# Gate row load moved, one weight block loaded in two pieces, ten weight blocks in one transfer: three edits to the loads of a fused mixing kernel

## The chip, the cores and the metric

The kernel runs on one core of one Trainium2 chip. Time is the device time of one execution in microseconds (us), as the median of several executions. Profiles are of one further execution each. A core has TensorE (matmuls, reading weights and data from the on-chip memory and adding up in eight banks of its own memory), VectorE, ScalarE and GpSimd, and SyncE, whose queue issues most loads. Sixteen DMA engines move the data.

## The reference, cut to what matters

```python
x = A_x                                          # 1 x 2048 x 512, bf16
g = sigmoid((x * gate_w).sum(-1, keepdims=True))
q, k, v = split_heads(x @ wqkv)                  # 32 heads of 16
phi = lambda t: concat(softmax(t @ w_phi), softmax(-(t @ w_phi)))
kv = einsum("bhsf,bhsd->bhfd", phi(k), v); z = phi(k).sum(s)
a = (phi(q) @ kv / (phi(q) @ z + 1e-6)) @ wo
b = relu(x @ w1) @ w2                            # w1 512 x 1376, w2 1376 x 512
return g * a + (1 - g) * b
```

## The kernel before

x is needed with its 512 columns on the partitions, in four chunks of 512 rows. Of chunk 0, TensorE transposes the first 256 columns itself and a transposing load brings the rest; chunks 1 to 3 come by transposing loads. The loads are issued in this order; `p.early` only moves the first ones ahead of the start's barrier.

```python
loadx0("sp", "x00", slice(0, 2), 0)
loadx0("act", "x01", slice(2, 4), 0)
p.dma("act", lambda e: e.dma_start(out=GR[0:NDT, :], in_=gate_w.rearrange("(j p) -> j p", p=P)),
      "gr", after=["grz"], ev="gr")               # the gate row, 1 KB
loadw1(0, 0, 4 * P, "a")                          # W1 block 0, columns 0..511
loadx0("sp", "x02", slice(0, 4), P)
loadw1(0, 4 * P, 8 * P)
for t in (1, 2):
    loadw1(t, 0, 8 * P)                           # W1 blocks 1 and 2, 256 KB each
p.dma("sp", ... e.dma_start_transpose(XT[:, 2:4, 0:512], ...), "x0t")     # chunk 0, columns 256..511
loadw1(3, 0, 8 * P)
p.dma("sp", ... W1[:, :, 8 * P:DFF] ..., "w1r")
p.dma("sp", ... WPS ... A_w_phi ..., "wps")       # w_phi, 16 KB
p.dma("sp", ... WV ..., "wv")                     # value weights, 512 KB
for i in range(2): p.dma("sp", ... e.dma_start_transpose(WQKT[...], ...), f"wqk{i}")  # query, key weights
for c in range(1, NCH): p.dma("sp", ... e.dma_start_transpose(XT[:, :, c * 512:...], ...), f"x{c}")
```

TensorE begins with the first MLP product of chunk 0 in four slabs. A slab takes one block of 128 columns of x and adds to all eight banks:

```python
XV = (("xva", "xvb"), ("xvc", "xvd"), ("x0t",), ("x0t",))
def slab(t, us=range(8)):
    for u in us:
        p.op("pe", lambda e, u=u: e.matmul(PS[:, UB[u], :], W1[:, t, u * P:(u + 1) * P], XT[:, t, 0:512], ...),
             after=["w10a" if t == 0 and u < 4 else f"w1{t}", *XV[t]] + ...)
```

Then it goes on in a fixed order, in which `hunit(1, 0)` is the first work on chunk 1. Everything ahead of it works on chunk 0 or on weights:

```python
hunit(0, 8); hunit(0, 9, "dve"); gatecol(0)
vtile(0, "dve"); vtile(1, "act", nextbank()); vtile(2, "dve")
for i in range(4): pre(i)              # folds w_phi into the query weights
vtile(3, "act", 5); rest(0); atile(0, 0)
for i in range(4, 8): pre(i)           # the same for the key weights
...
hunit(1, 0, "dve")                     # waits for "x1", rows 512..1023 of x
for m in range(NT): atile(m, None if m else 1); ...
    if m == 3:
        for a, b in ((0, 5), (5, KU)): # W2's whole blocks, 640 KB each
            p.dma("sp", ...)
```

The softmax here doesn't subtract the row's maximum and nothing guards it: scores larger than these inputs give would overflow.

## Time and profile before

| | before |
|---|---|
| median, three first runs | 146.74 us (146.73 to 147.30) |
| six runs beside the change | 146.78 us (146.67 to 147.30) |
| span of the profile | 145.3 us |
| TensorE busy | 98% |
| first W1 matmul / last matmul's weight load | 3.45 / 143.03 us |

SyncE's queue in order of time: start, length, queue and line, kind, tile, count.

```profile
3.10 1.34 SPq L176 DMA_TRANSPOSE XT<-in_A_x_dram  x1
...
5.57 0.51 SPq L181 DMA_DIRECT2D WPS<-in_A_w_phi_dram  x1
6.12 0.51 SPq L183 DMA_DIRECT2D WV<-in_A_wqkv_dram  x1
6.67 6.68 SPq L186 DMA_TRANSPOSE PHQ<-in_A_wqkv_dram  x2
13.39 7.58 SPq L189 DMA_TRANSPOSE XT<-in_A_x_dram  x3
```

Each line begins where the one above ends, give or take 0.05 us. These lengths are those of the issue; the data lands later.

### The profile page before, as it was taken

What the parts mean: (1) busy time and instruction counts of PE and PEld (TensorE: products, weight loads), DVE (VectorE), ACT (ScalarE), POOL (GpSimd) and SP (SyncE); (2) the same over time, 40 slices, a digit from 0 to 9 for tenths busy, and PEclk for the clock granted to TensorE, in tenths of its full rate; (3) what the DMA queues carried; (4) which work ended last, traced back from release to release, by engine and by line L of the source; (5) the groups of instructions that cost most, each with busy time, mean ns of one, the idle gap of its engine ahead of it and who ended that gap; (6) DMA issues with size and microseconds to landing.
All of it is one profiled execution on the core that took longest, in us unless ns stands there. A gap on an engine that the chain in (4) does not pass through costs nothing.

```text
span 145.3 us, 2523 instructions
## 1 busy us (share of the span) xinstructions
PE 142.3 (98%) x970; PEld 71.9 (50%) x970; DVE 92.5 (64%) x157; ACT 72.0 (50%) x125; POOL 52.1 (36%) x62
## 2 busy tenths in 40 slices
PE   8999999999999999999999999999999999999994
PEld 3444654454446445645555545554544444444443
DVE  3348557977686888678698968664455555555342
ACT  4124677778878778797878861122111111111150
POOL 2013002977878678678879801200000000000000
PEclk9999999999999999999999999999999999999999
DMA  6999994042359985315334332355142223222213
GB/s 153 250 299 201 251 202 89 0 94 55 72 119 355 154 167 109 70 36 111 77 72 103 78 72 40 80 104 134 49 108 72 72 72 77 72 72 74 72 45 106
DMA packets 47045, 16.12 MB, mean 111 GB/s; under 512 B 41432, under 2 KB 46648, under 8 KB 47032
## 3 DMA queue, kind: packets, MB, share of 16 engines
q1 hardware_dynamic: 46608, 15.85, 48.5%
q8 instruction: 8, 0.13, 0.4%
q10 hardware_dynamic: 424, 0.10, 0.3%
q14 instruction: 5, 0.04, 0.1%
HBM read 4.15 MB, written 2.10 MB: 43 GB/s over the span
## 4 chain that ended last, share of the span: by engine, by line
PE 94%; DMA 3%; DVE 1%; SPq 1%; issue 0%
PE PS L496 26%; PE PS L273 19%; PE PS L352 18%; PE PS L417 10%; PE PS L505 10%; PE PS L533 4%; PE PS L471 3%; PE PS L439 3%; DMA W<-in_B_w_dram 3%; PE PS L285 2%; PE PS L307 1%; DVE WQK L519 1%; SPq L162 0%; SPq L158 0%; PE PS L225 0%
## 5 line engine op out<-in xcount | busy, mean ns | idle before, releaser
L496 PE MATMUL PS<-W,HT 128*128 128x512 bf16 (+4 forms) x187 | 40.6, 366 | 0.0
L385 POOL TENSOR_TENSOR EB<-EB,SC 128x1024 bf16<-128x1024 bf16 x15 | 28.9, 1928 | 22.7 <-DVE SC L383 22.7
L336 ACT ACTIVATE EB<-PS 128x480 bf16<-128x480 f32 (+1 forms) x46 | 30.3, 732 | 13.4 <-PE PS L352 13.4
L510 ACT ACTIVATE TFA<-PS,GT 128x512 bf16<-128x512 f32 x16 | 11.0, 687 | 42.7 <-PE PS L505 36.6
L273 PE MATMUL PS<-XT,W 128*128 128x512 bf16 x128 | 30.9, 379 | 0.0
L352 PE MATMUL PS<-WQK,XT 128*128 128x480 bf16 x128 | 28.7, 366 | 0.0
L519 DVE SCALAR_TENSOR_TENSOR WQK<-PS,OMG,TFA 128x512 bf16<-128x512 f32 (+2 forms) x17 | 12.2, 719 | 23.6 <-ACT TFA L510 22.4
L496 PEld LDWEIGHTS PS<-W,HT 128*128 128x128 bf16 (+1 forms) x187 | 17.1, 98 | 17.4
L381 DVE TENSOR_REDUCE ZB<-EB 128x64 f32<-128x1024 bf16 x15 | 18.3, 1220 | 11.4 <-ACT EB L336 11.4
L259 ACT ACTIVATE HT<-PS 128x512 bf16<-128x512 f32 x34 | 19.8, 615 | 6.9 <-PE PS L533 5.1
L352 PEld LDWEIGHTS PS<-WQK,XT 128*128 128x128 bf16 x128 | 12.4, 98 | 13.8 <-DVE WQK L312 0.4
L396 DVE TENSOR_REDUCE ZB<-EB 128x64 f32<-128x1024 bf16 x16 | 18.6, 1164 | 0.0
L273 PEld LDWEIGHTS PS<-XT,W 128*128 128x128 bf16 x128 | 12.0, 98 | 13.0
L405 POOL TENSOR_TENSOR EB<-EB,SC 128x512 bf16<-128x512 bf16 x16 | 16.9, 1056 | 1.3
L417 PE MATMUL PS<-WV,XT 128*128 128x512 bf16 x64 | 16.2, 378 | 0.0
L505 PE MATMUL PS<-WO,OT 128*128 128x512 bf16 x64 | 16.1, 378 | 0.0
L481 DVE TENSOR_TENSOR WQK<-PS,RDEN 128x512 bf16<-128x512 f32 x16 | 11.1, 692 | 0.6
L427 ACT ACTIVATE VS<-PS 128x512 bf16<-128x512 f32 x14 | 8.5, 610 | 2.3 <-PE PS L417 2.3
L505 PEld LDWEIGHTS PS<-WO,OT 128*128 128x128 bf16 x64 | 6.1, 97 | 7.2
L383 DVE RECIPROCAL SC<-ZB 128x64 f32<-128x64 f32 x16 | 8.8, 553 | 0.5
L533 PE MATMUL PS<-XT,W 128*128 128x512 bf16 x32 | 7.5, 379 | 0.6 <-DMA W<-in_B_w_dram 0.3
L417 PEld LDWEIGHTS PS<-WV,XT 128*128 128x128 bf16 x64 | 5.4, 97 | 5.0 <-DVE VS L425 0.4
(57 smaller groups left out, 84.5 us busy)
## 6 DMA issues: line engine op xcount, KB each, us to landing
out_dram<-WQK SPq DMA_DIRECT2D x15, 128.0 KB, 1.8
W<-in_B_w_dram SPq DMA_DIRECT2D x2, 640.0 KB, 5.4
W<-in_B_w_dram SPq DMA_DIRECT2D x3, 256.0 KB, 3.8
WV<-in_A_wqkv_dram SPq DMA_DIRECT2D x1, 512.0 KB, 5.4
WO<-in_A_wo_dram SPq DMA_DIRECT2D x2, 256.0 KB, 3.4
W<-in_B_w_dram SPq DMA_DIRECT2D x1, 352.0 KB, 4.8
W<-in_B_w_dram SPq DMA_DIRECT2D x2, 128.0 KB, 2.5
PHQ<-EB SPq DMA_TRANSPOSE x16, 2.7
```

Source lines behind the costliest of these rows:

```text
L259: p.op("act", lambda e: e.activation(dst, src, ACT.Relu), after=[f"h{c}_{kt}"], ev=ev)
L273: p.op("pe", lambda e, t=t: e.matmul(PS[:, bank, :], W1[:, t, kt * P:(kt + 1) * P], XT[:, t, c * 512:(c + 1) * 512], start=(t == 0), stop= ...
L336: p.op("act", lambda e: e.activation(dst, s_, ACT.Exp, scale=scale), after=[qk] + busy, ev=ev)
L352: p.op("pe", lambda e, dt=dt, which=which: e.matmul(PS[:, which, 0:DE], XT[:, dt, m * P:(m + 1) * P], WQK[:, which, dt * DE:(dt + 1) * DE] ...
L381: p.op("dve", lambda e: e.tensor_reduce(zk, ek, AX.X, ALU.add), after=[emk, f"cst{b}"], ev=f"zk{m}")
L385: p.op("pool" if m < NT - 1 else "dve", lambda e: e.tensor_tensor(EB[:, b, 3, :].rearrange("p (g f) -> p g f", f=DH), EB[:, b, 2, :].rearr ...
L396: p.op("dve", lambda e: e.tensor_reduce(ZB[:, b, 0:64].rearrange("p (h s) -> p h s", s=2), bass.AP(tensor=EB, offset=base, ap=[[EBS, P], [ ...
L405: p.op("pool", lambda e: e.tensor_tensor(EB[:, b, 0, :].rearrange("p (h s f) -> p h s f", h=H, s=2)[:, :, 1, :], EB[:, b, 1, :].rearrange( ...
L417: p.op("pe", lambda e, dt=dt: e.matmul(PS[:, bank, :], XT[:, dt, m * P:(m + 1) * P], WV[:, dt, :], start=(dt == 0), stop=(dt == NDT - 1)), ...
L496: p.op("pe", lambda e, kt=kt, M=M: e.matmul(PS[:, bank, 0:n], HT[0:M, kt, m * P:(m + 1) * P], W2[0:M, kt, cs], start=(kt == 0), stop=(kt = ...
L505: p.op("pe", lambda e, t=t: e.matmul(PS[:, bank, :], OT[:, t, m * P:(m + 1) * P], WO[:, t, :], start=(t == 0), stop=(t == NDT - 1)), after ...
L519: p.op("dve", lambda e: e.scalar_tensor_tensor(out=OSB[:, ob, cs], in0=PS[:, bank, 0:n], scalar=OMG[:, m:m + 1], in1=TFA[:, m % 2, cs], op ...
```

## The change

The intent: the tiny gate row out of the way of the first loads; the first half of W1's second block early enough that slab 1 needn't wait; one issue less for W2.

```diff
-        p.dma("act", ... GR[0:NDT, :] ... gate_w ..., "gr", after=["grz"], ev="gr")     # at the start
...
-        for t in (1, 2):
-            loadw1(t, 0, 8 * P)
+        loadw1(1, 0, 4 * P, "a")
+        loadw1(1, 4 * P, 8 * P)
+        loadw1(2, 0, 8 * P)
...
-                    after=["w10a" if t == 0 and u < 4 else f"w1{t}", *XV[t]] + ...
+                    after=[f"w1{t}a" if t < 2 and u < 4 else f"w1{t}", *XV[t]] + ...
...
         xev("act", "b", (2, 3), (0,), 7)
+        p.dma("act", ... GR[0:NDT, :] ... gate_w ..., "gr", after=["grz"], ev="gr")
...
-                for a, b in ((0, 5), (5, KU)):
+                for a, b in ((0, KU),):
```

More of the change, by code (lines that the diff above doesn't have):

```diff
@@ L166, in bass_gated_mix__linear_kernel_hedgehog__dense_activation_relu__prompt_kernel @@
         loadx0("act", "x01", slice(2, 4), 0)
-        p.dma("act", lambda e: e.dma_start(out=GR[0:NDT, :], in_=gate_w.rearrange("(j p) -> j p", p=P)),
-              "gr", after=["grz"], ev="gr")
         p.early("act")
@@ L251, in xev @@
             free[bank] = [f"xv{nm}"]
-        w1all = ["w10a", "w1r"] + [f"w1{t}" for t in range(NDT)]
+        w1all = ["w10a", "w11a", "w1r"] + [f"w1{t}" for t in range(NDT)]
         def relu(c, kt, bank, eng):
@@ L535, in slab @@
                     start=(t == 0), stop=(t == NDT - 1)),
-                    after=["w10a" if t == 0 and u < 4 else f"w1{t}", *XV[t]] + (free[UB[u]] if t == 0 else []),
+                    after=[f"w1{t}a" if t < 2 and u < 4 else f"w1{t}", *XV[t]] + (free[UB[u]] if t == 0 else []),
                     ev=(f"h0_{u}" if t == NDT - 1 else None))
@@ L545, in bass_gated_mix__linear_kernel_hedgehog__dense_activation_relu__prompt_kernel @@
         xev("act", "b", (2, 3), (0,), 7)
+        p.dma("act", lambda e: e.dma_start(out=GR[0:NDT, :], in_=gate_w.rearrange("(j p) -> j p", p=P)),
+              "gr", after=["grz"], ev="gr")
         warm(1, 384)
```

## The prediction

> **What bounds the kernel now.** I read the page's shares and chain first, to see which engine sets the end; then the chain in order of time, to see what comes ahead of that engine's stream; then the timeline of the first 23 us; then the DMA issues of short windows, because all three parts of the change are loads.
>
> ```profile
> PE 142.3 (98%) x970; PEld 71.9 (50%) x970; DVE 92.5 (64%) x157; ACT 72.0 (50%) x125; POOL 52.1 (36%) x62
> ...
> PE 94%; DMA 3%; DVE 1%; SPq 1%; issue 0%
> ```
>
> TensorE is busy for 98% of the span and is 94% of the chain that ended last; only 3% of the chain is a DMA. So a load can pay only where TensorE really stands still, and this is at the start. The chain in order of time, from the beginning, shows the one load on it:
>
> ```profile
> 1.60 0.51 SPq L162
> 2.11 0.04 issue
> 2.15 3.71 DMA W<-in_B_w_dram
> 5.86 0.05 issue
> 5.90 5.45 PE PS L533 x24
> ```
>
> The 2.15 us issue is the second block of W1 (rows 128 to 255, columns 0 to 1023, 256 KB), which slab 1 waits for. It landed 3.71 us later, at 5.86. The timeline gives the size of the hole:
>
> ```profile
> 2.92 0.38 ACT L250 ACTIVATE XT<-PS 128x256 bf16<-128x256 f32 x1 [0.22 <-PE PS L238]
> 3.45 0.81 PE L533 MATMUL PS<-XT,W 128*128 128x512 bf16 x3 [0.24 <-ACT XT L250]
> 4.32 1.24 PE L533 MATMUL PS<-XT,W 128*128 128x512 bf16 x5
> 5.90 5.45 PE L533 MATMUL PS<-XT,W 128*128 128x512 bf16 x24 [0.34 <-DMA W<-in_B_w_dram]
> 7.71 3.15 PEld L533 LDWEIGHTS PS<-XT,W 128*128 128x128 bf16 x16 [0.40 <-issue]
> ...
> 19.67 1.03 PE L273 MATMUL PS<-XT,W 128*128 128x512 bf16 x4
> ```
>
> A matmul of 512 columns is shown as 0.38 us long, but the starts of these follow each other every 0.216 us, so I count from starts. The last matmul of slab 0 starts at 5.18; the next could start at 5.40 and starts at 5.90: **0.50 us lost**. Slab 2's first matmul starts at 7.74 where 7.64 was free: 0.10 us lost. I added up every start-to-start distance from 3.45 us to the tail beyond columns/2.4 ns: only four exceed it by over 25 ns, 0.51, 0.10, 0.09 and 0.10 us. The last two (14.75 and 20.63 us) wait for evacuations that follow TensorE's own work. From 3.45 us on there is thus at most about 0.6 us for this change to win, 0.4% of the time.
>
> The hole at 7.64 matters most. Slab 2 needs columns 256 to 511 of x, transposed by the load issued at 3.10 us, and the third W1 block, issued at 2.63. Three queries of the DMA issues in windows at 2.15, at 3.1 and at 13.4 us answer, one line from each:
>
> ```profile
> W<-in_B_w_dram SPq DMA_DIRECT2D x1, 256.0 KB, 3.7
> XT<-in_A_x_dram SPq DMA_TRANSPOSE x1, 4.5
> XT<-in_A_x_dram SPq DMA_TRANSPOSE x1, 6.1
> ```
>
> The first is W1's second block. The second: 3.10 + 4.5 = 7.60, so the transposing load of x lands 0.04 us before slab 2 was free to begin and 0.14 us before it began. W1's third block landed at 6.56 by its semaphore's record, a microsecond earlier. So **slab 2 already hangs on the transposed x**, not on W1. The third line is the transposing load of x's rows 512 to 1023: 13.39 + 6.1 = 19.49, and the first matmul that reads them starts at 19.67. These are two appointments that TensorE meets with under 0.2 us to spare.
>
> **What the Trainium skill says.** "Perfetto Trace Analysis", section "DMA Optimizations", says that splitting a DMA lets some of it start sooner if the DMA engines are otherwise idle, and that larger ones use bandwidth better. Here the engines are not idle: the page's slices show 0.9 of them busy from the second to the fifth slice, and from 3.2 us on the packet records show 13 to 16 or more packets in flight at any time. "DMA: Bandwidth & Descriptors", section "Issuing engines are not separate DMA queues", says that DMAs from ScalarE and SyncE run on the same 16 engines, and another queue saves only the sequencer's time. The trace agrees as far as both queues (q1, q10) have packets in the same microsecond. The same page, section "Why a DMA increments its semaphore by 16 and not by 1", says that every engine used adds its share and only the full count means landed. The trace bears this out: of the 16 increments of W1's second block, 11 came from 4.44 to 4.77 us and the last five from 5.49 to 5.86. The hole before slab 1 is those five stragglers; some packets of 2 KB took 0.5 to 1.27 us there where the median is 0.084.
>
> **The change part by part.**
>
> Gate row. Its issue holds ScalarE's queue for 0.62 us (0.69 to 1.31); without it the table load of 1.28 us starts some 0.65 us earlier. But ScalarE's first evacuation at 2.92 us waits for the transposes on TensorE (released by line 238, which ended at 2.89), not for the table, which was loaded at 2.71. And those transposes began at 2.30 because their x pieces landed at 2.16. Gain: 0. The row is 1 KB; TensorE reads it at 12.91 us, so landing some microseconds after 2.68 costs nothing. ScalarE's next evacuation starts at 4.41, 1.1 us after the first ended at 3.31, room for a 0.62 us issue. Removing it may ease the first W1 piece (landed 3.19), which isn't what slab 0 waits for last: ScalarE's evacuation ended at 3.31.
>
> W1's second block in two. The first 128 KB now holds what the first four matmuls of slab 1 need. With the measured rate of 0.25 MB in the microsecond the fast shares land near 4.3; even with the straggler the first piece should come by about 5.2. Slab 1 then begins at 5.40, 0.50 us earlier. The four later matmuls, from 6.27, need the second piece, which held till 5.86 as part of the whole. Local gain 0.50 us. Slab 1 then is done at 5.40 + 8 x 0.216 = 7.13, where slab 2 stands before the transposed x. If this still lands at 7.60, slab 2 begins at 7.74 as now: the 0.50 us come back as a wait of 0.60. Added cost: one issue of 0.43 to 0.51 us on SyncE ahead of that transposing load. It moves it from 3.10 to about 3.57. I estimate what that costs from a transposing load with an uncrowded queue: 256 KB from 27.89 us on took 2.7 us to land. So 3.57 + 2.7 = 6.3 is the earliest; 7.6 is set by the data queued before it. Nearly all of the delay should hide. Packets of 1 KB instead of 2 KB cost 46 against 84/2 = 42 ns per KB, over 16 KB for each engine about 0.06 us.
>
> W2 in one. Two issues of 0.57 and 0.52 us at 40.9 us become one, of perhaps 0.6 to 1.1. The same bytes land by about 48 us and are first read at 87.4; the next issue on SyncE comes 1.5 us later and waits for another engine. Nothing of it is on TensorE's path. Gain 0.
>
> Sum: 0.50 won before slab 1, about 0.50 given back before slab 2, 0 to 0.1 for finer packets: 0.0 net.
>
> **The rivals.**
>
> First: the stragglers go. The transposing load stood still on 13 engines from 5.54 to 6.36 us, single packets of 256 B taking 0.7 to 0.83 us, until the last W1 packets ended at about 6.14. Finer pieces could spread the slow packets; then this load could land up to 0.8 us earlier, and slab 2 begin at 7.13. For it: the stall plainly waits for late engines. Against it: total bytes are the same, and the next appointment is at 19.49 us. If that load comes earlier with the rest, 0.6 us are won: 146.1. If it doesn't, TensorE waits there, and almost nothing is: 146.7.
>
> Second: the extra issue is not hidden. The transposing loads follow each other on SyncE without a pause (6.68 to 20.97 us). If the 0.47 us pass through, slab 2 and the rows at 19.49 come 0.4 to 0.5 us later: 147.2. For it: 19.67 has almost no slack. Against it: the issues of the later transposing loads last 2.0 to 4.6 us where an uncrowded one takes 1.2, so SyncE is waiting for the data engines and the backlog should absorb the delay.
>
> Third: the gate row's issue, now in the middle of the loads, holds ScalarE past 4.41 and delays the transposed x of slab 1. A delay under 0.5 us would again only fill the wait before slab 2. It changes 146.7 by nothing unless it is over a microsecond.
>
> **Range and chances.** No net change, 146.7, gets 45%; some earlier landing, 146.1 to 146.6, 30%; a later one, 146.9 to 147.3, 25%. Weighted, the middle is about 146.65. The three runs before spread from 146.73 to 147.3, so another 0.2 us on top for runs: 146.2 to 147.2. Two per cent is 2.9 us, five times all that the start has to give: within 2% at 98%.
>
> **What would show it right or wrong.** Right: slab 1's first matmul near 5.4 us, and a new wait of some 0.4 to 0.6 us before slab 2, ended by the transposed x near 7.6; the x rows of the second 512 still landing about 19.5 with matmuls right behind; from there to the end the same 123 us; ScalarE's first evacuation still released by TensorE at about 2.9. Wrong: slab 2 at 7.1 and the 19.67 us matmul earlier too, which is the first rival; slab 2 after 8.0, the second; ScalarE's second evacuation after 5 us, the third. Only a change after 20 us, where I expect none, would bring a figure outside the range.

## The result, and the profile after

| | before | changed |
|---|---|---|
| median of 6 runs | 146.78 us (146.67 to 147.30) | 147.53 us (147.13 to 147.91) |
| ratio | | 1.0045, 95% interval 1.0023 to 1.0067 |
| span of the profile | 145.3 us | 145.8 us |

Ratios here and below are the mean time of one kernel's fast runs over that of the other's fast runs of the same rounds, so not quite the ratio of the medians. The change made the kernel a little slower, and the time lies outside the predicted range of 146.2 to 147.2.

The page of the changed kernel, shares and chain:

```profile
PE 142.2 (98%) x953; PEld 72.5 (50%) x970; DVE 92.5 (63%) x157; ACT 72.0 (49%) x125; POOL 52.1 (36%) x62
...
PE 97%; issue 1%; DVE 1%; ACT 0%; DVEq 0%
```

The load has left the chain, as intended, and still the kernel is slower. (953 matmuls instead of 970 are missing records; all 970 weight loads are there, so below I place things by weight loads.) The chain in order of time says what took its place:

```profile
2.92 0.39 ACT XT L249
3.31 0.14 issue
3.45 1.44 PE PS L532 x3
4.88 0.43 PE PS L237 x4
5.31 6.59 PE PS L532 x29
```

The first three W1 matmuls begin at 3.45 us as before, but take 1.44 us instead of 0.81. Their starts are 0.38 and 0.43 us apart instead of 0.216. **TensorE runs at half speed here, until 5.9 us**; before, it ran at full speed from 3.45 on. Slab 2's first weight load thus came at 8.07 instead of 7.71 us. The granted clock on the page is full throughout in both, so it doesn't tell of this. The trace's own clock records do: full clock began at 3.48 us before and at 5.86 us after. They lasted 143.360 and 139.946 us, 3.414 us apart; that is 42 and 41 times 3.413 us.

The second thing to see is SyncE's queue after:

```profile
3.58 1.33 SPq L175 DMA_TRANSPOSE XT<-in_A_x_dram  x1
...
6.04 0.51 SPq L180 DMA_DIRECT2D WPS<-in_A_w_phi_dram  x1
6.59 0.51 SPq L182 DMA_DIRECT2D WV<-in_A_wqkv_dram  x1
7.15 7.49 SPq L185 DMA_TRANSPOSE PHQ<-in_A_wqkv_dram  x2
14.68 7.07 SPq L188 DMA_TRANSPOSE XT<-in_A_x_dram  x3
```

From the transposed x of chunk 0 to the query weights every issue is 0.47 us later, and the one for chunk 1 is 1.29 us later (14.68 against 13.39). That load took 5.6 us to land instead of 6.1, so it landed at 20.25 instead of 19.49. In TensorE's timeline the first matmuls on chunk 1 come right behind (the record of the first of the four is missing; its weight load began at 20.30):

```profile
19.39 1.00 PE L306 MATMUL PS<-Wbd,PHQ 128*128 128x120 bf16 x16
20.53 0.81 PE L272 MATMUL PS<-XT,W 128*128 128x512 bf16 x3
```

TensorE had stood for less than 0.15 us before that weight load, because the slow start had made it late already. So one profile offers two causes: a slow start of TensorE's clock, and chunk 1 landing late. The first may be chance, the second may be the change. One profile can't tell.

### The profile page after: what moved, and what is told of

The parts are those of the page before. It is cut to its first block, busy times and chain, and to the rows that moved or that the text cites. A ratio compares the mean times of both kernels' runs of the same rounds, so it can differ in the third digit from the quotient of the medians.

```text
span 145.8 us, 2506 instructions
## 1 busy us (share of the span) xinstructions
PE 142.2 (98%) x953; PEld 72.5 (50%) x970; DVE 92.5 (63%) x157; ACT 72.0 (49%) x125; POOL 52.1 (36%) x62
## 4 chain that ended last, share of the span: by engine, by line
PE 97%; issue 1%; DVE 1%; ACT 0%; DVEq 0%
PE PS L495 25%; PE PS L272 19%; PE PS L351 18%; PE PS L504 9%; PE PS L416 9%; PE PS L532 6%; PE PS L470 3%; PE PS L438 3%; PE PS L284 2%; PE PS L231 1%; PE PS L306 1%; DVE WQK L518 1%; PE PS L237 1%; ACT XT L249 0%; DVE ONE L207 0%
## 5 line engine op out<-in xcount | busy, mean ns | idle before, releaser
L495 PE MATMUL PS<-W,HT 128*128 128x512 bf16 (+3 forms) x182 | 40.2, 366 | 0.3
L416 PE MATMUL PS<-WV,XT 128*128 128x512 bf16 x60 | 15.5, 379 | 0.2
```

The source lines that it names most:

```text
L416: p.op("pe", lambda e, dt=dt: e.matmul(PS[:, bank, :], XT[:, dt, m * P:(m + 1) * P], WV[:, dt, :], start=(dt == 0), stop=(dt == NDT - 1)), ...
L495: p.op("pe", lambda e, kt=kt, M=M: e.matmul(PS[:, bank, 0:n], HT[0:M, kt, m * P:(m + 1) * P], W2[0:M, kt, cs], start=(kt == 0), stop=(kt = ...
```

## The experiments

Theories at the outset: **C**, the clock comes up at a random time, and the change only lays it bare; **S**, the extra issue on SyncE delays all later loads; **G**, the gate row's packets among W1's loads hurt. All 18 runs gave correct results and were timed in five rounds, in five groups, each on one chip. Each group has its own runs of the kernel before, except the second: of its twelve, eleven are those of the first group, on the same chip some ten minutes earlier.

### The change part by part

`e1_gate` moves the gate row alone, `e2_w1split` splits W1's block alone, `e3_w2one` joins W2 alone, `e4_all` is the whole change again; each diff is that part of the diff above.

> Only the gate row's load moved behind ScalarE's first evacuation. Theory C (the warm-up of TensorE's clock falls at a random time, and the change lays it bare): no reliable difference, ratio 0.998 to 1.002. Theory G (the gate row's small packets in the middle of W1's loads hurt): ratio 1.003 to 1.005. Theory S (the extra issue on SyncE hurts): ratio 1.000.

> Only W1's second block loaded in two column pieces. Theory S (one more issue ahead of all later loads makes the rows at 19.5 us land later, and the matmuls at 19.7 us wait): ratio 1.003 to 1.006, with that landing past 19.9 us. Theory C: 0.998 to 1.002 on average, with the warm-up anywhere from 3.3 to 6 us. Theory G: 1.000.

> Only W2's ten whole blocks in one transfer. All theories: ratio 0.999 to 1.001, nothing of it on TensorE's path. Its profile is a further sample of the old start: under theory C its warm-up time differs from the 3.4 us of the kernel before.

> The whole change once more, for the size of the slowdown and a second profile. Theories G and S: ratio 1.003 to 1.006 again. Theory C: the profile shows a warm-up at another time than 5.6 us, and the time of slab 2 follows it; if the warm-up is before 4.5 us, the profiled span is 145.0 to 145.4.

| | median us | ratio (95%) |
|---|---|---|
| before, 11 runs | 147.05 | |
| gate row alone | 147.02 | 0.9995 (0.9977 to 1.0013) |
| split alone | 147.44 | 1.0024 (1.0003 to 1.0045) |
| W2 alone | 147.07 | 1.0001 (0.9983 to 1.0019) |
| whole change | 147.51 | 1.0035 (1.0006 to 1.0064) |

G falls: the gate row shows no effect beyond the interval's 0.2%, and neither does W2. The split alone carries most of it by its middle value, 0.24 of 0.35%, which is a little under what S expected (1.003 to 1.006). In the profile of the split the chain of waits in order of time shows the path; L184 issues the value weights, L187 the query and key weights, and the DMA is chunk 1:

```profile
6.60 0.51 SPq L184
7.11 0.04 issue
7.15 4.96 SPq L187
12.11 0.04 issue
12.15 2.62 SPq L187
14.77 0.04 issue
14.81 6.21 DMA XT<-in_A_x_dram
21.02 0.05 issue
21.07 1.04 PE PS L274 x4
```

The chain runs through SyncE's queue, issue behind issue, to chunk 1's landing at 21.02 and TensorE 0.05 us later. TensorE stood idle before it, here in the timeline of this profile; and in the profile of W2 alone, which has the old start, it waited for the same load too, only for less:

```profile
21.07 1.04 PE L274 MATMUL PS<-XT,W 128*128 128x512 bf16 x4 [1.35 <-DMA XT<-in_A_x_dram]
```

```profile
20.19 1.04 PE L273 MATMUL PS<-XT,W 128*128 128x512 bf16 x4 [0.38 <-DMA XT<-in_A_x_dram]
```

In this profile of the split the clock was up before 3.5 us, and yet the span was 146.6 us; so theory C alone can't explain the slowdown. Slab 1 began early, so the profile also shows the prediction's give-back before slab 2:

```profile
4.24 2.97 PE L534 MATMUL PS<-XT,W 128*128 128x512 bf16 x13
7.62 1.24 PE L534 MATMUL PS<-XT,W 128*128 128x512 bf16 x5 [0.42 <-DMA XT<-in_A_x_dram]
```

Slabs 0 and 1 run without a break, and then the transposed x of chunk 0 ends an idle time of 0.42 us.

### One issue more, one issue less

Is it the extra issue, or the smaller packets of the split block (rival **P**)?

```diff
 # f1_dummy: kernel before, a load of 128 x 32 bytes to nowhere, ahead of W1's block 1
+p.dma("sp", lambda e: e.dma_start(out=DUM[:, :], in_=B_w1[0:P, 0:16]), "dum", ev="dum")
 # f2_piece_act: split, but the second piece is issued by ScalarE behind its first evacuation
-loadw1(1, 4 * P, 8 * P)
+loadw1(1, 4 * P, 8 * P, eng="act")
 # f3_wps_act: kernel before, w_phi's load issued by ScalarE behind its first evacuation
-p.dma("sp", ... WPS ...)
+p.dma("act", ... WPS ...)
 # f4_all_wps_act: the whole change with f3's edit
```

> The kernel before with one small extra load (128 rows of 32 bytes) on SyncE ahead of W1's second block; no block is split. Theory S (one more issue of some 0.45 us delays every later load on SyncE, and the x rows that landed at 19.5 to 20.1 us land 0.5 to 0.8 later): ratio 1.002 to 1.005, those rows past 20.2 us. Rival P (the smaller packets of the split block, or its extra completion, slow the data engines): ratio 0.999 to 1.001.

> The split kept, but its second piece is issued by ScalarE behind its first evacuation, so SyncE issues as many loads as before. Theory S: ratio 0.998 to 1.001, x rows at 19.5 to 20.2 us. Rival P: ratio 1.002 to 1.004 as for the split alone.

> The kernel before with the small load of w_phi (issue of 0.51 us on SyncE, 512 packets of 32 bytes) given to ScalarE behind its first evacuation: one issue less ahead of the transposing loads. Theory S: the x rows land about 19.0 to 19.6 us, ratio 0.996 to 0.999, not more, because TensorE is then itself the bound at 19.6. Rival P: ratio 0.999 to 1.001.

> The whole change, with w_phi's load given to ScalarE too: SyncE issues as many loads as before. Theory S: ratio 0.998 to 1.001, x rows at 19.5 to 20.2. Rival P: 1.002 to 1.005, as the whole change.

| | issues on SyncE ahead of chunk 1, against before | median us | ratio (95%) | chunk 1 landed |
|---|---|---|---|---|
| before, 12 runs | 0 | 147.06 | | |
| small extra load | +1 | 147.19 | 1.0015 (0.9994 to 1.0035) | 20.03 |
| piece from ScalarE | 0 | 147.25 | 1.0013 (0.9996 to 1.0030) | 20.13 |
| w_phi from ScalarE | -1 | 146.86 | 0.9985 (0.9969 to 1.0002) | 19.02 |
| whole change, w_phi from ScalarE | 0 | 146.93 | 0.9987 (0.9969 to 1.0005) | 19.20 |

Every interval includes 1, so no single row decides. The last row says most: the whole change with one issue taken off SyncE is at 0.9987, with all its small packets, where P said 1.002 to 1.005 and the whole change in the group before was at 1.0035, on the same chip and against nearly the same runs of the kernel before. That speaks for S and against P. The first two rows fit neither. S said 1.002 to 1.005 for the small load and 0.998 to 1.001 for the piece from ScalarE, P said 0.999 to 1.001 and 1.002 to 1.004; both came out between, and the second kept half of the split's excess. Their landings say little here: both profiles are of the fastest of six runs.

### Making it worse: four pieces

```diff
+for i in range(3): loadw1(1, 2 * i * P, 2 * (i + 1) * P, "abc"[i])
+loadw1(1, 6 * P, 8 * P)          # g4_four: three issues more instead of one
```

> W1's second block in four column pieces: three issues more on SyncE instead of one. Theory S (each issue ahead delays the later loads by its own length): the x rows land 1.4 to 2 us later than with no split (21.3 to 22.2 us), ratio 1.009 to 1.014. If the data engines' backlog hides the issues, 1.000 to 1.003.

The ratio was 1.0055 (1.0027 to 1.0083), 148.09 us against 147.21, under the expected 1.009 to 1.014; the landing, at 22.33, was later than the expected range. That the time fell short and the landing ran over is no contradiction: the landing is that of the profiled execution alone. In this execution, which was the slowest of its runs (149.19 us), the timeline shows the wait:

```profile
22.38 1.04 PE L275 MATMUL PS<-XT,W 128*128 128x512 bf16 x4 [1.58 <-DMA XT<-in_A_x_dram]
```

### Wanting chunk 1 later

If the end hangs on chunk 1, TensorE should do something else first. Its order allows it: fold the query and key weights one V tile earlier, and do the postponed V tile and tile 0's keys ahead of `hunit(1, 0)`. Chunk 1 is then wanted a microsecond later, and no load is touched.

```diff
-vtile(0, "dve"); vtile(1, "act", nextbank()); vtile(2, "dve")
+vtile(0, "dve"); vtile(1, "act", nextbank())
 for i in range(4): pre(i)
 ...
-hunit(1, 0, "dve")
+vtile(2, "dve", nextbank())       # first try; mended: vtile(2, "dve", 5)
-mid = [[(1, 1)], ...
+mid = [[(1, 0), (1, 1)], ...      # now behind tile 0's keys
```

> The kernel before with TensorE's work reordered and no load touched: the V tile of rows 256 to 383 moves behind the folding of the key weights, and tile 0's keys come ahead of the first matmuls on x rows 512 to 1023, which are then wanted at 20.6 us instead of 19.7. Theory B (the end hangs on the landing of these rows, at 19.5 to 20.1 us in the old order, and on the warm-up of TensorE's clock): the wait goes, ratio 0.997 to 0.999. Rival N (the end doesn't hang on this landing): 1.000 or more.

> The whole change with the same reordering of TensorE's work. Theory B: the rows land as late as in the whole change (20.2 to 21.0 us) but are wanted a microsecond later, so most of the 0.35 to 0.45% goes: ratio 0.998 to 1.001, and the difference to the reordered kernel before is under 0.2%. Rival N: still 1.003 to 1.005 over the reordered kernel before.

> The reordered kernel before, with w_phi's load given to ScalarE as well: a candidate to beat both kernels. Theory B: nothing at 19 to 21 us waits for a load any more, ratio 0.996 to 0.999, no better than the reordering alone by over 0.1%.

All three came out slow: 1.0033, 1.0040 and 1.0020. This was a fault of mine. `nextbank` hands out banks in turn, and one call more shifted every later bank. In all three profiles the product that begins the last stage found its bank still being emptied by ScalarE, as here in `g1_order`:

```profile
88.69 1.67 PE L496 MATMUL PS<-W,HT 128*128 128x512 bf16 x7 [0.53 <-ACT HT L259]
```

By starts this cost 0.69 us. The mended version gives the moved tile bank 5 and leaves the rotation alone. It ran beside the whole change on one chip:

> The reordering of TensorE's work on the kernel before, mended: the moved V tile takes bank 5 and leaves the rotation of banks as it was, so the wait of 0.69 us at 88 us that the first try brought in goes. Theory B (the end hangs on the landing of the x rows or on the clock's warm-up): ratio 0.997 to 0.9995. Rival N: 1.000 to 1.002.

> The whole change with the mended reordering. Theory B: the rows still land at 20.0 to 21.0 us, and the time is within 0.15% of the mended reordering of the kernel before, 0.3 to 0.5% under the whole change of the same rounds. Rival N: it stays 0.3 to 0.5% over the reordered kernel before.

> The mended reordering with w_phi's load given to ScalarE. Theory B: as the mended reordering, within 0.1%, ratio 0.996 to 0.999: the loads are early enough and only the clock's warm-up and W1's second block are left.

> The whole change beside these on the same chip. Theory B: ratio 1.003 to 1.005, the x rows landing at 20.2 to 21 us, and the first matmul on them within 0.06 us of the later of that landing and TensorE's own chain.

| | median us | ratio (95%) |
|---|---|---|
| before, 11 runs | 147.17 | |
| before, reordered | 146.83 | 0.9975 (0.9958 to 0.9992) |
| whole change, reordered | 146.98 | 0.9985 (0.9970 to 1.0001) |
| before, reordered, w_phi from ScalarE | 146.92 | 0.9995 (0.9976 to 1.0015) |
| whole change | 147.32 | 1.0009 (0.9986 to 1.0032) |

**In this group the reordered kernel before is faster than both kernels.** It is the only one of the three reorderings whose interval lies clear of 1: the third was expected within 0.1% of it and came out 0.2% higher. In the profile of the first, chunk 1 landed as late as 20.61 us, and TensorE's matmuls came to it later still, at 20.84, without a wait:

```profile
20.04 0.97 PE L352 MATMUL PS<-WQK,XT 128*128 128x480 bf16 x4
20.84 1.89 PE L273 MATMUL PS<-XT,W 128*128 128x512 bf16 x8
```

But as a test of the cause it is weak: here the whole change was only 0.09% over before, not the expected 0.3 to 0.5%, and the reordering brought it down by 0.24%, not by 0.3 to 0.5%. Hence the last pair, four pieces with and without the reordering.

> W1's second block in four pieces, with the mended reordering. Theory B (the cost of extra issues runs through the wait for the x rows): the four pieces make that wait sure to be there, so wanting the rows a microsecond later gives back nearly the whole microsecond: 0.8 to 1.0 us (0.5 to 0.7%) under the four pieces without it, against 0.25% for the reordering where the wait is there only in some executions. Rival N: no more than the 0.25% again.

> W1's second block in four pieces, on the same chip as its reordered twin: ratio 1.005 to 1.010, x rows at 21.8 to 22.6 us.

Without it 147.89 us, ratio 1.0038 (1.0014 to 1.0062); with it 147.51, ratio 1.0018 (0.9985 to 1.0051). The ratio without it is again under the expected one, and chunk 1 landed at 21.09 in its profile, earlier than the expected 21.8 to 22.6. The reordering gave back 0.38 us, not the 0.8 to 1.0 that I expected. That is 0.26%, the figure of rival N, so the number of this pair doesn't speak for theory B. The profile of the reordered one shows what was left, by starts: 0.25 us before the folding of the query weights, which landed at 15.30 and are now wanted at 15.1, and 0.42 us for chunk 1, which in this execution landed at 21.54. So TensorE still stood for chunk 1: the wait was moved in part, not removed.

### All profiles side by side

Thirteen profiles have TensorE's old order. "Slow until" is the start that ends the last distance at half speed, the transposing matmuls of 128 columns included; for e3_w2one and i2_four, which have no full distance at half speed, it is the start of full clock by the clock record. "Slab 2" is its first weight load.

| kernel | issues | slow until | slab 2 | chunk 1 landed | first weight load on chunk 1 | span | span less that |
|---|---|---|---|---|---|---|---|
| before | 0 | under 3.5 | 7.71 | 19.49 | 19.62 | 145.26 | 125.64 |
| changed | +1 | 5.91 | 8.07 | 20.25 | 20.30 | 145.82 | 125.52 |
| e1_gate | 0 | 6.03 | 8.19 | 20.09 | 20.30 | 145.95 | 125.65 |
| e2_w1split | +1 | under 3.5 | 7.59 | 21.02 | 21.06 | 146.59 | 125.53 |
| e3_w2one | 0 | 3.70 | 7.68 | 20.14 | 20.18 | 145.71 | 125.53 |
| e4_all | +1 | 5.09 | 7.76 | 20.70 | 20.74 | 146.26 | 125.52 |
| f1_dummy | +1 | 3.83 | 7.92 | 20.03 | 20.07 | 145.59 | 125.52 |
| f2_piece_act | 0 | 4.24 | 7.80 | 20.13 | 20.17 | 145.66 | 125.49 |
| f3_wps_act | -1 | under 3.5 | 7.72 | 19.02 | 19.64 | 145.28 | 125.64 |
| f4_all_wps_act | 0 | 5.46 | 8.59 | 19.20 | 20.50 | 146.15 | 125.65 |
| g4_four | +3 | 4.18 | 8.66 | 22.33 | 22.37 | 147.90 | 125.53 |
| h4_all | +1 | under 3.5 | 7.95 | 20.98 | 21.02 | 146.55 | 125.53 |
| i2_four | +3 | 3.59 | 8.09 | 21.09 | 21.14 | 146.67 | 125.53 |

The last column is the same within 0.16 us in all of them. **Everything that differs happens before TensorE reaches chunk 1.** In nine of the thirteen it reaches it 0.04 to 0.05 us after the landing, having stood still for it, from under 0.1 us (changed) to 1.74 us (g4_four) by starts. In the other four (before, e1, f3, f4) its own chain is later than the landing, and in e1 and f4 this is a slow start of the clock, in f4 with a late transposed x as well. The 0.1 us between 125.5 and 125.65 is the evacuation wait at 20.63 us, which a wait for chunk 1 hides.

With the seven reordered profiles too, there are twenty landings of chunk 1. By issues more or fewer on SyncE they are on average: -1, 19.45 (3 profiles); 0, 19.86 (7); +1, 20.48 (7); +3, 21.65 (3). That is 0.4 to 0.6 us for each issue. The value weights landed at 11.26, 11.76, 12.17 and 13.14 on average, 0.4 to 0.5 us for each issue, which is the length of an issue, 0.43 to 0.51. Single profiles lie up to 0.75 us off these averages: with 0 extra issues from 19.20 to 20.61.

Nor are these executions the median ones. The profile of g4_four is of the slowest of its seven runs, those of the changed kernel, f1_dummy and f2_piece_act are of the fastest of six, and the one of the kernel before, at 146.55 us, is of an execution faster than every timed run of that kernel. As the rest is constant, a run's time can stand in for a profile: in the thirteen, the time less the first weight load on chunk 1 is 126.8 to 126.95 us. My estimate from this is that the median runs of f1_dummy and f2_piece_act reached chunk 1 near 20.4 us, not near 20.1, and those of g4_four and i2_four near 21.3 and 21.1. By these medians three more issues cost 0.88 and 0.51 us, that is 0.2 to 0.3 us each, less than the landings of the few profiles say.

## Why the prediction was wrong

It said 146.65 (its own three chances and middles give 146.70) and a range up to 147.2; measured were 147.53 in its own rounds and, in two further groups, ratios of 1.0035 and 1.0009.

- **The step that failed** stands in "The change part by part": the extra issue moves the transposing load to 3.57, and "Nearly all of the delay should hide", with chunk 1 "still landing about 19.5". For the transposed x of chunk 0 it was right: it landed at 7.23 to 7.84 in six profiles with the split on SyncE and at 8.48 in one, 7.43 to 8.02 in the eight with that block whole and nothing added ahead. For the loads behind it was wrong. With one issue more the value weights landed 0.41 us later on average and chunk 1 0.62 us later, and chunk 1 is what TensorE waits for.
- **Why it didn't hide.** I took the long issues of the transposing loads (2.0 to 4.6 us) for slack that would shrink. If so, the first, for the query weights, should have become shorter by the delay; it lasted 4.82 us on average in the seven profiles of unchanged issue count and 4.78 in the seven with one more. In all twenty profiles that issue ended 0.14 to 0.31 us before the value weights landed, and the value weights' landing moved with their own issue. This suggests that SyncE was held by a load whose time also hung on SyncE. The Trainium skill, "Perfetto Trace Analysis", section "What "DMA-bound" means", names an issuing queue that is solid with DMA slices as one of the things that can bind. This trace was exactly that from 1.60 to 20.97 us; I had seen it and argued it away. What exactly holds the transposing issue is not shown.
- **The second rival named it**, with 147.2 us and too small a weight. Its size was off too: it counted 0.4 to 0.5 us for the rows, where one more issue went with 0.6, and it started from the one profile before, in which chunk 1 landed at 19.49, early among the seven of unchanged issue count (mean 19.86). And e3_w2one, whose loads up to there are those of the kernel before, had a wait of 0.38 us for chunk 1 in its profile. So an execution without the split can wait for chunk 1 too; how many do is not shown.
- **Slab 1 and the give-back** were right where the clock was up in time: in e2_w1split and h4_all slab 1 began at 5.1 to 5.3 us and slab 2 waited, ended by the transposed x at 7.49 and 7.84. The first rival, 0.6 us won, didn't happen. The two signs set for the other rivals, slab 2 after 8.0 us and ScalarE's second evacuation after 5 us, did show in the first profile after, at 8.07 and 5.13, but both through the slow clock.
- **A missing term: the clock.** I counted from 216 ns at 3.45 us as a fact of the kernel. Over twenty profiles with the same opening on TensorE the half speed ended anywhere from under 3.5 to 6.03 us. Changed and unchanged kernels have both ends (e2_w1split and h4_all under 3.5, changed 5.91; before under 3.5, e1_gate 6.03), so nothing ties it to the change. It explains the 0.36 us by which slab 2 was late in the first profile after, and gives no reason why the medians should differ. The Trainium skill, "TensorE: Matmul & The Clock Gate", section "Part 1: The HAM clock gate (the "warmup" mystery)", says that the window that lets the clock go up is 3.413 us long and doesn't restart with the kernel, so that the same kernel varies from run to run. The traces agree: in the nine profiles that hold a record of the full clock it lasted 41 or 42 times that length, and the end of the half speed spreads over at least 2.5 us.
- **Gate row and W2** were right: 0.9995 and 1.0001. (The prediction overlooked that W2's last 96 KB are issued right behind, at 42.06 us; nothing on TensorE hung on it.) The gate row's issue began at 2.92 us, together with the evacuation that it stands behind in the program, not after it, and ScalarE's second evacuation at 5.13 waited for TensorE, not for the issue: the third rival is out.

**What is shown and what stays open.** Shown: the split alone makes the kernel slower, if by little (1.0003 to 1.0045); in the split's profiles with a fast clock TensorE stops for chunk 1's landing, and after it all kernels with the old order take the same time. Argued: that it is the extra issue and not the smaller packets (the whole change with one issue taken off SyncE speaks for it, the small extra load and the piece from ScalarE decide nothing), and the 0.6 us for each issue, which is from averages of few profiles and more than the medians say. Open: why the piece issued by ScalarE kept half the excess; what moves chunk 1 from one execution to the next by as much as the change does; and why the whole change cost 0.45, 0.35 and 0.09% in three groups. There the medians of the changed kernel were 147.53, 147.51 and 147.32 us and those of the kernel before 146.78, 147.05 and 147.17, so it is the kernel before that moved more.

## What to carry to other kernels

When an issuing queue is busy without a break, an extra issue can be paid by loads far behind it, even where the next load hides it: here the transposed x of chunk 0 landed no later, and chunk 1 did. So its cost is to be read at the last load that somebody waits for, not at the one beside the split. Look for the next appointment before filling a hole: here 0.5 us won at 5.4 us could never pass the loads due at 7.6 and 19.5. And where a landing makes its appointment by 0.2 us in one profile, take several profiles before building on it, and see how fast the profiled execution was among the runs. Letting TensorE do other work first is a way out that touches no load; it gave 0.25% in one of three variants here, and whether it beats moving the loads is not shown.

## What the Trainium skill lacked or had wrong

- "Perfetto Trace Analysis", section "DMA Optimizations", advises splitting a DMA where the engines are idle, and doesn't give its price on the issuing queue: here 0.43 to 0.51 us of issue, and chunk 1's landing later by some 0.6 us with one issue more (20.48 against 19.86 on average of seven profiles each) and 1.8 with three more (21.65, three profiles), though by the medians of the runs three more cost 0.5 to 0.9 us. A length of the issue stands only in "DMA: Bandwidth & Descriptors", in cycles of the sequencer and for "previous generations".
- No page says that the issue of a transposing load can last until the plain load ahead of it has nearly landed. "Perfetto Trace Analysis" counts a wait for the descriptor generator into the profiled issue, without a word on how long it can be. In all twenty profiles the issue for the query weights ended 0.14 to 0.31 us before that landing, after 4.3 to 5.6 us of issue for 512 KB.
- "TensorE: Matmul & The Clock Gate" has the random warm-up right; but it gives a variation of 0.5 us either way for the time at which the clock goes up. Here it went from under 3.5 to 6.03 us over twenty profiles with the same opening on TensorE. (The page's own count of 6, 11 or 14 slow matmuls for one kernel allows for more than its 0.5 us.)
